# The normalized input of chunks 5 to 7: loaded with columns on partitions and normed on VectorE, in place of transposes on TensorE

## The chip, the cores and the metric

The kernel runs on one core of a Trainium2 chip. The metric is the device time of one execution in microseconds; the time before is the median of three runs. In what follows TensorE is written PE in the profile's rows, VectorE DVE, ScalarE ACT, GpSimd POOL, and SyncE (which here only issues DMAs) SP.

## The reference

A layer norm of the input goes into two branches, and their sum and the input are the result. One branch is a long causal convolution with a gate, the other a dense layer with Mish between two matrix products.

```python
x = A_q                                   # 1 x 2048 x 448
xn = _layernorm(x, axis=-1)               # (x - mean) / sqrt(var + 1e-5)
return x + _A_ref(xn, A_k, A_v, A_shift_k, A_ssm_k, A_ssm_D) + _B_ref(xn, B_w1, B_b1, B_w2)

# A: k_shift = 4-tap causal convolution of k;  kv = k_shift * v
#    y = causal convolution of kv with ssm_k over 2048 steps + kv * ssm_D;  return xn * y
# B: h = xn @ w1 + b1                       # 448 -> 1792
#    return (h * tanh(softplus(h))) @ w2    # 1792 -> 448
```

## The kernel before

**The dense branch** is cut into 8 chunks of 256 tokens, and each chunk into 7 pairs of 128 hidden units. A pair is two slots. In the even slot `g1_mm` multiplies the first layer (L466), in the odd slot `mish` (L469) applies Mish on ScalarE, rounds the result to `ach` and has VectorE subtract the rest, `acl` (L74), and `g2_mm` (L493 to L495) adds the second layer of the pair two earlier to PSUM. Every product is made of rounded high and low parts, 22 matmuls in a first layer and 12 in a second. Chunk c is normalized while chunk c-1 runs, and `g2_evac` (L500) adds the second layer's PSUM to the chunk's own input and SP stores it (L505).

**The norm of a chunk** starts from tokens on partitions: `ln_load` fetches the chunk into `qt`, `ln_stats` queues two `bn_stats`, two `bn_aggr` and the addition of eps for VectorE, and POOL makes 1/sqrt (L395) and the shift. These five small steps are not put in at once: each `dv()` in the program takes one from the list `drip`, so they come between VectorE's other instructions, and what is left is flushed two pairs before the chunk ends. `ln_norm` norms on ScalarE into `xn` (L402), and `ln_T` has TensorE transpose a half of the chunk into PSUM (four matmuls with an identity, L427), ScalarE round it to `XH` (L439) and VectorE subtract the rest, `XL` (L437). The first half is done in the odd slot of pair 5 ahead of that pair's Mish, the second in the even slot of pair 6.

**The convolution branch** is a Fourier transform in two steps of 64 and 32 points, a product and the way back, and its pieces are put into the slots by a table. `f1_mm` (L127) is the 64-point step, `f1_fold` its VectorE part (`st`, L134 and L136), and ScalarE stores the result to `Dkv`. From slot 63 on eight octets follow: SP loads `ah` and `av` back, `h2_mm` and `v2_mm` (L201) are the 32-point step, ScalarE copies their PSUM to `hs` and `vs`, VectorE multiplies (`prod`: `ya`, `yb`, `yc`, `yd`, L234), `i1_mm` (L244) goes back, and `qe` is stored to `E`. From slot 98 on `E` is loaded again (`e`), VectorE folds it (L287, L289), `i2_mm` (L305) makes the result and `gate` multiplies it with the normalized input. `h2_mm`, `v2_mm` and `i1_mm` share two PSUM tiles `pc`, so each waits for ScalarE's copies of the one before.

**The order** on each engine is that of the program; nothing is reordered. Pieces named with `at` come ahead of the dense branch's part of a slot, those with `after` behind it, and `inside` puts some between Mish and `ach` where a transpose shares the slot. A DMA that reads what an earlier DMA wrote waits for its landing on the queue of the engine that issues it, and what stands behind it on this engine waits too.

Of the kernel before, what the change touches and what calls it, by code (L numbers as in the profile page):

```python
# [7 lines left out]
F32 = mybir.dt.float32  # L8
# [6 lines left out]
S, D, F = 2048, 448, 1792  # L15
NJ = 16
NF = F // 128
NP = NF // 2
CH = 256
NCHUNK = S // CH  # L20
# [7 lines left out]
OCT_AT = (65, 3)  # L28
I2_AT = {98: (6, 7), 102: (0, 1), 106: (2, 3), 109: (4, 5)}
LATE = 2  # L30
WARM = (448,) * 4 + (128,)
FILL = ((64,), (128, 128))


@with_exitstack
def tile_kernel(ctx: ExitStack, tc, q, k, v, sk, hT, sD, w1, b1, w2, c_f1, c_g, c_gi, c_i2, out):
    nc = tc.nc
    V = nc.vector

    def pool(name, bufs=1, stack=ctx, **kw):  # L40
        return stack.enter_context(tc.tile_pool(name=name, bufs=bufs, **kw))

    cp = pool("consts")
    wp = pool("weights")
    mp = pool("mlp")
# [3 lines left out]
    dp = pool("scratch", space=DRAM)  # L49
# [4 lines left out]
    Dkv = dp.tile([NO * 16, 32, D], F32, name="Dkv")  # L54
    E = dp.tile([2, 2, 32, 2, NCHUNK, 2, D], F32, name="E")

    f1id = cp.tile([128, 2, 128], F32, name="f1id")
    f1, ident = f1id[:, 0], f1id[:, 1]
    mhalf = cp.tile([128, 2], F32, name="mhalf")
    b1t = cp.tile([128, NF], F32, name="b1t")  # L60
    mv = cp.tile([128, NJ, 2], F32, name="mv")
    rstd = cp.tile([128, NJ], F32, name="rstd")
# [9 lines left out]
    def split(h, l, raw):  # L72
        nc.scalar.copy(h, raw)  # L73
        V.tensor_sub(l, raw, h)  # L74
# [2 lines left out]
        return pcp.tile([128, 2, 512], F32, name="pc")  # L77


    drip = []  # L80

    def dv(n=1):
        for _ in range(n):
            if drip:
                drip.pop(0)()


    plan, plan2, plan3 = {}, {}, {}
# [5 lines left out]
        plan2.setdefault(int(slot), []).append((fn, args))  # L94

    def inside(slot, fn, *args):
        (plan3 if slot % 2 and slot // 2 % NP == NP - 2 else plan2).setdefault(int(slot), []).append((fn, args))


    ph1 = ExitStack()  # L100
    sp1 = pool("ph1", stack=ph1)
    skb = sp1.tile([128, 4, D], F32, name="skb")
    HT, KR, VT, KV, PS, ST, SD = {}, {}, {}, {}, {}, {}, []

    def xt():
# [70 lines left out]
    def t2(shape, name, bufs=1):  # L176
        if not sp2:
            ph1.close()
            sp2.append(ph2.enter_context(tc.tile_pool(name="ph2", bufs=1, reuse_waits="tile")))
        return sp2[0].tile(shape, F32, name=name, bufs=bufs)  # L180
# [85 lines left out]
    def t3(shape, name, bufs=2):  # L266
        if not sp3:
            ph2.close()
            sp3.append(ph3.enter_context(tc.tile_pool(name="ph3", bufs=2, reuse_waits="tile")))
            i2 = sp3[0].tile([128, 2, 32], F32, name="i2", bufs=1)  # L270
            nc.sync.dma_start(i2, c_i2)
            sp3.append(i2)
        return sp3[0].tile(shape, F32, name=name, bufs=bufs)

    def late(c):
        return c >= NCHUNK - LATE

# [88 lines left out]
    XS, XN, NORM = {}, {}, {}  # L366

    def ln_load(c, eng=None):
        Q[c] = mp.tile([128, 2, D], F32, name="qt", tag="qt", bufs=3)
        if c:  # L370
            nc.sync.dma_start(Q[c], q[:, 2 * c:2 * c + 2])
        else:
            for jj in range(2):
                nc.sync.dma_start(Q[c][:, jj], q[:, jj])

    def ln_parts(c):
        st = mp.tile([128, 2, 6], F32, name="bst", bufs=2)
        ve = mp.tile([128, 2], F32, name="ve", bufs=2)
        xn = mp.tile([128, 2, D + 64], F32, name="xn", tag="xn", bufs=1)
        XN[c] = xn  # L380

        def stats(jj):
            V.bn_stats(st[:, jj], Q[c][:, jj])  # L383

        def aggr(jj):
            V.bn_aggr(mv[:, 2 * c + jj], st[:, jj])  # L386

        def eps(a, b):
            V.tensor_scalar(ve[:, a:b], mv[:, 2 * c + a:2 * c + b, 1], EPS, None, op0=ALU.add)

        def power(a, b):
            r, m = (t[:, 2 * c + a:2 * c + b] for t in (rstd, shift))
            if c:
                nc.gpsimd.tensor_tensor(m, mv[:, 2 * c + a:2 * c + b, 0], mone[:, a:b], op=ALU.mult)  # L394
            nc.gpsimd.tensor_tensor(r, ve[:, a:b], mhalf[:, a:b], op=ALU.pow)  # L395
            if c:
                nc.gpsimd.tensor_tensor(m, m, r, op=ALU.mult)

        def norm(jj):
            j = 2 * c + jj  # L400
            if c:
                nc.scalar.activation(xn[:, jj, :D], Q[c][:, jj], AF.Identity, bias=shift[:, j:j + 1],  # L402
                                     scale=rstd[:, j:j + 1])
            else:
                V.tensor_scalar(xn[:, jj, :D], Q[c][:, jj], mv[:, j, 0:1], rstd[:, j:j + 1],
                                op0=ALU.subtract, op1=ALU.mult)

        def tail(a, b):
            (nc.scalar.copy if c else V.tensor_copy)(xn[:, a:b, D:], xn[:, a:b, D - 64:D])

        return stats, aggr, eps, power, norm, tail

    def ln_stats(c):
        stats, aggr, eps, power, norm, tail = ln_parts(c)
        drip.extend([lambda: stats(0), lambda: stats(1), lambda: aggr(0), lambda: aggr(1),
                     lambda: [eps(0, 2), power(0, 2)]])
        NORM[c] = norm, tail

    def ln_norm(c):
        norm, tail = NORM.pop(c)  # L420
        norm(0)
        norm(1)
        tail(0, 2)

    def transposes(c, jj, p):
        for kt in range(4):
            nc.tensor.transpose(p[:, 128 * kt:128 * kt + 128], XN[c][:, jj, 128 * kt:128 * kt + 128], ident)  # L427

    def x_tiles(c):
        XS[c] = (mp.tile([128, 4, CH], F32R, name="XH", tag="XH", bufs=2),  # L430
                 mp.tile([128, 4, CH], F32R, name="XL", tag="XL", bufs=2))
# [9 lines left out]
    def ln_T(c, jj):  # L441
        if jj == 0:
            x_tiles(c)
        p = g1p.tile([128, 2, CH], F32, name="pg1").rearrange("p a b -> p (a b)")
        transposes(c, jj, p)
        for lo in range(2):
            x_split(c, jj, p, lo)
# [5 lines left out]
    def g1_mm(i):  # L453
        c, p = pairs[i]
        XH, XL = XS[c]
        ps = g1p.tile([128, 2, CH], F32, name="pg1")
        for n in range(2):
            f = 2 * p + n
            fs = slice(128 * f, 128 * f + 128)
            mm = []  # L460
            hh, hl, lh = ([(w[:, kt, fs], x[:, kt]) for kt in range(3)] for w, x in ((w1h, XH), (w1h, XL), (w1l, XH)))
            th, tl = ((w1h[:, 3, fs], x[:, 3]) for x in (XH, XL))

            mm = hh + hl + lh + [th, tl] if i == 0 and n else hh + lh + [th] + hl + [tl]
            for n_, (l, r) in enumerate(mm):
                nc.tensor.matmul(ps[:, n], l, r, start=n_ == 0, stop=n_ == len(mm) - 1)  # L466
        P1[i] = ps

    def mish(i, s):  # L469
        p = pairs[i][1]  # L470
        ps = P1.pop(i)
        a = mp.tile([128, 2, CH], F32, name="a", bufs=2)
        for n in range(2):
            nc.scalar.activation(a[:, n], ps[:, n], AF.Mish, bias=b1t[:, 2 * p + n:2 * p + n + 1])  # L474
        for fn, args in plan3.pop(s, ()):
            fn(*args)
        ah = mp.tile([128, 2, CH], F32R, name="ach", bufs=3)
        al = mp.tile([128, 2, CH], F32R, name="acl", bufs=3)
        split(ah, al, a)
        dv()  # L480
        AHL[i] = ah, al
# [25 lines left out]
    def mlp_slot(s):  # L507
        i, half = divmod(s, 2)
        n = len(pairs)
        j = i - G2_LAG  # L510
        if half == 0:
            if i < n:
                c, p = pairs[i]
                if c + 1 < NCHUNK:
                    if p == (0 if c else 1):
                        ln_load(c + 1)
                    if p == (2 if c else 3):
                        ln_stats(c + 1)
                    if c == 0 or p == NP - 3:
                        dv(len(drip))  # L520
                    if p == NP - 2:
                        ln_norm(c + 1)
                    if p == NP - 1:
                        ln_T(c + 1, 1)
                g1_mm(i)
        else:
            if i < n:
                c, p = pairs[i]
                if p == NP - 2 and c + 1 < NCHUNK:
                    ln_T(c + 1, 0)  # L530
                mish(i, s)
            if 0 <= j < n - 1:
                g2_mm(j)
            elif j == n - 1:
                for jj in range(2):
                    g2_mm(j, (jj,))
                    g2_evac(pairs[j][0], (jj,))
# [71 lines left out]

    heat(WARM)  # L610
    ln_load(0)
    nc.scalar.dma_start(f1id, c_f1)
    w1_load(0, ((0, 1, nc.scalar), (1, 2, nc.sync)))
# [26 lines left out]
    for s in range(nslots):  # L640
        j = s // 2 - G2_LAG - 1
# [70 lines left out]
```

## Time and profile before

| | |
|---|---|
| median of 3 runs | 372.51 us (372.32 to 373.36) |
| the profiled execution | 372.71 us, its span 370.3 us |
| instructions | 7465 |
| granted clock of TensorE | 1.000 |

The span runs from the first to the last instruction, and the 2.4 us between it and the execution's own time lie around it. The page cuts the span into 40 slices of 9.26 us; a digit is the busy share in tenths.

```profile
DVE  5798758999999998997432848555384822897741
ACT  4777553543426323533454556557555435235450
DMA  8899989747587427614876497877493329649963
```

VectorE is full up to about 175 us (the taps and the 64-point steps), less so where the octets run, and busy again from 312 us on. In a timeline a row gives the start in us, the length, the engine (PEq, ACTq, SPq for what only issues), the line, what is written and read, and in brackets how long the engine stood idle before it and for whom. Lengths of matmuls overlap: the distance between two starts is what a matmul takes of TensorE. In the list of DMA issues the last number is the time from issue to landing.

### The profile page before, as it was taken

Reading aid. Unit: us, or ns where it says so; the run is one execution under the profiler, and the core shown is the slowest. Engines: PE = TensorE matmul, PEld = TensorE weight load, DVE = VectorE, ACT = ScalarE, POOL = GpSimd, SP = SyncE. Lnnn points to the kernel's source line nnn. Section 1 sums busy time; section 2 is a strip of 40 time slices with the busy share of each in tenths; the row PEclk is TensorE's granted clock in tenths of the full one; section 3 lists DMA queues with packets and bytes.
Section 4 is the critical chain, followed back from the end, with each engine's and each line's share of the span. In section 5 each row is a group of like instructions: output and inputs, shape, how many; then the busy total and the mean of one; then the engine's idle time right before and its main releaser. Section 6 shows DMA issues by size and latency. Waiting matters only on the chain.

```text
span 370.3 us, 7465 instructions
## 1 busy us (share of the span) xinstructions
PE 363.7 (98%) x3136; PEld 294.4 (80%) x3136; DVE 265.8 (72%) x356; ACT 177.0 (48%) x298; POOL 21.9 (6%) x38
## 2 busy tenths in 40 slices
PE   8999999999999999999999999999999999999995
PEld 3888888888888988988886666666666879889884
DVE  5798758999999998997432848555384822897741
ACT  4777553543426323533454556557555435235450
POOL 2010001000020001000010000020000010112110
PEclk9999999999999999999999999999999999999999
DMA  8899989747587427614876497877493329649963
GB/s 285 285 321 337 396 288 270 181 152 238 148 273 228 100 54 247 169 32 99 264 237 218 139 301 239 264 240 242 167 298 116 149 104 364 226 180 298 226 106 94
DMA packets 32354, 79.35 MB, mean 214 GB/s; under 512 B 2881, under 2 KB 18114, under 8 KB 32322
## 3 DMA queue, kind: packets, MB, share of 16 engines
q1 hardware_dynamic: 25986, 57.39, 45.4%
q10 hardware_dynamic: 4896, 15.08, 15.0%
q0 software_dynamic: 1440, 6.42, 7.0%
q8 instruction: 24, 0.39, 0.5%
q14 instruction: 8, 0.07, 0.0%
HBM read 50.44 MB, written 28.44 MB: 213 GB/s over the span
## 4 chain that ended last, share of the span: by engine, by line
PE 83%; DVE 8%; DMA 5%; ACT 1%; issue 1%; POOL 0%; SPq 0%; ACTq 0%
PE pg L466 34%; PE pg L493 11%; PE pg L495 10%; PE pg L494 10%; PE pc L201 7%; PE pc L127 4%; PE pc L244 3%; PE pg L427 2%; PE pc L305 2%; DMA kr<-in_k_dram 2%; DMA Dkv<-st 1%; DMA av<-Dkv 1%; DMA qt<-in_q_dram 1%; DVE x L165 1%; DVE bst L383 1%
## 5 line engine op out<-in xcount | busy, mean ns | idle before, releaser
L474 ACT ACTIVATE a<-pg,b1t 128x256 f32<-128x256 f32 x112 | 47.1, 473 | 108.4 <-PE pg L466 85.0
L466 PE MATMUL pg<-XH,w1h 128*128 128x256 f32 x448 | 91.3, 285 | 0.2
L493 PE MATMUL pg<-w2h,ach 128*128 128x448 f32 x224 | 83.6, 373 | 0.2 <-DVE qt L500 0.2
L466 PEld LDWEIGHTS pg<-XH,w1h 128*128 128x128 f32 x448 | 69.7, 188 | 17.3 <-issue 14.3
L495 PE MATMUL pg<-w2h,acl 128*128 128x448 f32 x224 | 81.3, 363 | 0.0
L494 PE MATMUL pg<-w2l,ach 128*128 128x448 f32 x224 | 81.2, 362 | 0.0
L74 DVE TENSOR_TENSOR acl<-a,ach 128x512 fp32r<-128x512 f32 x56 | 38.5, 687 | 58.7 <-ACT ach L73 58.5
L466 PE MATMUL pg<-XL,w1h 128*128 128x256 f32 x448 | 69.8, 278 | 0.0
L466 PEld LDWEIGHTS pg<-XL,w1h 128*128 128x128 f32 x448 | 59.6, 188 | 0.1
L466 PE MATMUL pg<-XH,w1l 128*128 128x256 f32 x336 | 57.0, 278 | 0.0
L493 PEld LDWEIGHTS pg<-w2h,ach 128*128 128x128 f32 x224 | 42.0, 187 | 14.0 <-issue 9.7
L466 PEld LDWEIGHTS pg<-XH,w1l 128*128 128x128 f32 x336 | 47.0, 188 | 0.0
L495 PEld LDWEIGHTS pg<-w2h,acl 128*128 128x128 f32 x224 | 42.1, 188 | 2.8
L494 PEld LDWEIGHTS pg<-w2l,ach 128*128 128x128 f32 x224 | 42.1, 188 | 2.2
L73 ACT CAST ach<-a 128x512 fp32r<-128x512 f32 x56 | 34.8, 622 | 1.7
L165 DVE TENSOR_TENSOR x<-x 128x896 f32<-128x896 f32 x24 | 26.2, 1090 | 0.8
L439 ACT CAST XH<-pg 128x512 fp32r<-128x512 f32 x16 | 9.4, 588 | 26.5 <-PE pg L427 24.2
L437 DVE TENSOR_TENSOR XL<-pg,XH 128x512 fp32r<-128x512 f32 x16 | 10.9, 684 | 14.4 <-ACT XH L439 14.3
L133 ACT COPY st<-pc 128x896 f32<-128x896 f32 x16 | 14.5, 906 | 13.3 <-PE pc L127 13.3
L134 DVE TENSOR_TENSOR st<-pc,st 128x896 f32<-128x896 f32 x16 | 17.4, 1086 | 4.2 <-ACT st L133 4.0
L394 POOL TENSOR_TENSOR shift<-mv,mone 128x2 f32<-128x2 f32 x7 | 2.8, 397 | 277.9 <-DVE mv L386 277.9
L252 ACT COPY qe<-pc 128x896 f32<-128x896 f32 x16 | 13.8, 913 | 10.8 <-PE pc L244 10.8
(65 smaller groups left out, 392.1 us busy)
## 6 DMA issues: line engine op xcount, KB each, us to landing
Dh<-st ACTq DMA_DIRECT2D x16, 448.0 KB, 5.5
Dkv<-st ACTq DMA_DIRECT2D x16, 448.0 KB, 4.9
ah<-Dh SPq DMA_DIRECT2D x8, 896.0 KB, 6.4
av<-Dkv SPq DMA_DIRECT2D x8, 896.0 KB, 5.4
E<-qe SPq DMA_DIRECT2D x16, 448.0 KB, 3.7
kr<-in_k_dram SPq DMA_DIRECT2D x10, 448.0 KB, 6.1
x<-in_hT_dram SPq DMA_DIRECT2D x8, 448.0 KB, 6.7
x<-in_v_dram SPq DMA_DIRECT2D x8, 448.0 KB, 4.1
```

The source lines that it names most:

```text
L73: nc.scalar.copy(h, raw)
L74: V.tensor_sub(l, raw, h)
L127: nc.tensor.matmul(ps[h][64 * jj:64 * jj + 64, b, :D], f1[rg:rg + 32, 0:64], x[rg:rg + 32, jj], start=True, stop=True, tile_position=(rg, ...
L133: nc.scalar.copy(st[:, 1], o)
L134: V.tensor_add(st[:, 0], e, st[:, 1])
L165: V.tensor_add(KV[g], KV[g], o)
L201: nc.tensor.matmul(p[32 * t:32 * t + 32, r, :D], g[rs, t, c], a[rs, t], start=True, stop=True, tile_position=(64 * r, 32 * t))
L466: nc.tensor.matmul(ps[:, n], l, r, start=n_ == 0, stop=n_ == len(mm) - 1)
L474: nc.scalar.activation(a[:, n], ps[:, n], AF.Mish, bias=b1t[:, 2 * p + n:2 * p + n + 1])
L493: nc.tensor.matmul(ps, ah[:, n, cs], w2h[:, f], start=f == 0, stop=False)
L494: nc.tensor.matmul(ps, ah[:, n, cs], w2l[:, f], start=False, stop=False)
L495: nc.tensor.matmul(ps, al[:, n, cs], w2h[:, f], start=False, stop=f == NF - 1)
```

## The change

Chunks 5, 6 and 7 (`TURN = 5`, `turned(c)`) get their normalized input on another way.

- The input `qx`, made ahead of the launch as a copy of the three chunks with columns on partitions (128 partitions x 4 groups x 256 tokens, 512 KB for a chunk), is loaded by SP into the buffer of `xn`, ahead of `qt`. The chunk is still loaded as `qt` too, for the statistics and for `g2_evac`.
- The statistics are queued one pair earlier (pair 1 in place of 2) and flushed one pair earlier (pair 3 in place of 4). POOL's two shift instructions are left out.
- In the odd slot of pair 3, `ms_store` has ScalarE's queue store mean and 1/sqrt of the 256 tokens to `MS` in memory, two DMAs of 128 x 2 single values. In the odd slot of pair 4, `ms_load` loads them back to all 128 partitions as `bc` (128 x 512, 256 KB). Both stand ahead of the slot's Mish.
- In the odd slot of pair 5, behind Mish and `acl`, `x_norm` subtracts the mean and multiplies by 1/sqrt on VectorE, two instructions of 128 x 1024. In the even slot of pair 6, `x_cast` rounds to `XH` on ScalarE (one instruction of 128 x 1024) and subtracts to `XL` on VectorE (one of 128 x 1024).
- The 24 transposes, the three times three instructions of `ln_norm` and the twelve half-size `XH` and `XL` are gone. The `hs` or `qe` copies that stood between Mish and `ach` in pair 5 now stand behind the slot.
- The transform's matrix and the identity move to a memory pool that is closed before the octets start.

```diff
+TURN = 5
...
+    MS = dp.tile([NCHUNK, 2, CH], F32, name="MS")
...
     def inside(slot, fn, *args):
-        (plan3 if slot % 2 and slot // 2 % NP == NP - 2 else plan2).setdefault(int(slot), []).append((fn, args))
+        c, p = divmod(slot // 2, NP)
+        (plan3 if slot % 2 and p == NP - 2 and not turned(c + 1) else plan2).setdefault(int(slot), []).append((fn, args))
...
     def ln_load(c, eng=None):
+        if turned(c):
+            XN[c] = mp.tile([128, 4, CH], F32, name="xt", tag="xn", bufs=1)
+            nc.sync.dma_start(XN[c], qx[:, c - TURN])
...
+    def ms_store(c):
+        for i, t in enumerate((mv[:, 2 * c:2 * c + 2, 0], rstd[:, 2 * c:2 * c + 2])):
+            nc.scalar.dma_start(MS[c, i].rearrange("(j p) -> p j", p=128), t)
+
+    def ms_load(c):
+        BC[c] = t3([128, 2, CH], "bc", 1) if c == NCHUNK - 1 else t2([128, 2, CH], "bc")
+        nc.scalar.dma_start(BC[c], MS[c].partition_broadcast(128))
+
+    def x_norm(c):
+        for i, op in enumerate((V.tensor_sub, V.tensor_mul)):
+            op(XN[c], XN[c], BC[c][:, i:i + 1].to_broadcast([128, 4, CH]))
+
+    def x_cast(c):
+        x_tiles(c)
+        split(*XS[c], XN[c])
...
-                    if p == (2 if c else 3):
+                    if p == ((1 if turned(c + 1) else 2) if c else 3):
                         ln_stats(c + 1)
-                    if c == 0 or p == NP - 3:
+                    if c == 0 or p == (NP - 4 if turned(c + 1) else NP - 3):
                         dv(len(drip))
-                    if p == NP - 2:
+                    if turned(c + 1):
+                        if p == NP - 1:
+                            x_cast(c + 1)
+                    elif p == NP - 2:
                         ln_norm(c + 1)
-                    if p == NP - 1:
+                    elif p == NP - 1:
                         ln_T(c + 1, 1)
...
-                if p == NP - 2 and c + 1 < NCHUNK:
+                t = turned(c + 1) and c + 1 < NCHUNK
+                if t and p == NP - 4:
+                    ms_store(c + 1)
+                if t and p == NP - 3:
+                    ms_load(c + 1)
+                if p == NP - 2 and c + 1 < TURN:
                     ln_T(c + 1, 0)
                 mish(i, s)
+                if t and p == NP - 2:
+                    x_norm(c + 1)
```

The order moves at three places that the prediction speaks of. In these rows a line number of the changed program is 7 to 28 higher than before for the same statement.

The first is VectorE in slots 59 to 62, where chunk 5 is being prepared: `acl` is the dense branch's subtraction, `qt` the emptying of chunk 3's second layer, `st` the last 64-point step, `bst`, `mv` and `ve` the statistics of chunk 5. Before:

```order
L74 TENSOR_TENSOR acl<-a,ach 128x512 x2
L500 TENSOR_TENSOR qt<-pg_1653,qt 128x448
L500 TENSOR_TENSOR qt<-pg_1657,qt 128x448
L134 TENSOR_TENSOR st<-pc,st 128x896
L383 BN_STATS bst<-qt 128x6
L136 TENSOR_TENSOR st<-pc,st 128x896
L383 BN_STATS bst<-qt 128x6
L74 TENSOR_TENSOR acl<-a,ach 128x512
```

Now:

```order
L75 TENSOR_TENSOR acl<-a,ach 128x512 x2
L393 BN_STATS bst<-qt 128x6
L528 TENSOR_TENSOR qt<-pg_1654,qt 128x448
L393 BN_STATS bst<-qt 128x6
L528 TENSOR_TENSOR qt<-pg_1658,qt 128x448
L396 BN_AGGR mv<-bst 128x2
L141 TENSOR_TENSOR st<-pc,st 128x896
L396 BN_AGGR mv<-bst 128x2
L143 TENSOR_TENSOR st<-pc,st 128x896
L399 TENSOR_SCALAR ve<-mv 128x2
```

Both statistics have moved from between the folds to ahead of the second add.

The second is VectorE in slots 87 to 90, with octet 7's product (`ya` to `yc`), the emptying of chunk 5 and the statistics of chunk 7. Before:

```order
L74 TENSOR_TENSOR acl<-a,ach 128x512
L234 TENSOR_TENSOR ya<-vs,hs 128x896
L234 TENSOR_TENSOR yb<-vs,hs 128x896
L234 TENSOR_TENSOR ya<-ya,yb 128x896
L500 TENSOR_TENSOR qt<-pg_2694,qt 128x448
L500 TENSOR_TENSOR qt<-pg_2698,qt 128x448
L234 TENSOR_TENSOR yc<-vs,hs 128x896
L383 BN_STATS bst<-qt 128x6
L234 TENSOR_TENSOR yd<-vs,hs 128x896
L383 BN_STATS bst<-qt 128x6
L234 TENSOR_TENSOR yc<-yc,yd 128x896
L386 BN_AGGR mv<-bst 128x2
```

Now:

```order
L393 BN_STATS bst<-qt 128x6
L241 TENSOR_TENSOR ya<-vs,hs 128x896
L393 BN_STATS bst<-qt 128x6
L241 TENSOR_TENSOR yb<-vs,hs 128x896
L396 BN_AGGR mv<-bst 128x2
L241 TENSOR_TENSOR ya<-ya,yb 128x896
L396 BN_AGGR mv<-bst 128x2
L528 TENSOR_TENSOR qt<-pg_2691,qt 128x448
L399 TENSOR_SCALAR ve<-mv 128x2
L528 TENSOR_TENSOR qt<-pg_2695,qt 128x448
L241 TENSOR_TENSOR yc<-vs,hs 128x896
L241 TENSOR_TENSOR yd<-vs,hs 128x896
```

All of the statistics, the aggregations and eps too, have come ahead of the last `yc`.

The third is VectorE in slots 93 to 97, where chunk 7 is made ready and chunks 6 and 7 of the convolution are folded (`ex`, `e`). Before:

```order
L437 TENSOR_TENSOR XL<-pg_3536,XH 128x4x128
L74 TENSOR_TENSOR acl<-a,ach 128x512
L287 TENSOR_TENSOR ex<-e_3500 128x896
L289 TENSOR_TENSOR e_3500<-e_3500 128x896
L287 TENSOR_TENSOR ex<-e_3502 128x896
L289 TENSOR_TENSOR e_3502<-e_3502 128x896
L437 TENSOR_TENSOR XL<-pg_3570,XH 128x4x128
L74 TENSOR_TENSOR acl<-a,ach 128x512
```

Now:

```order
L75 TENSOR_TENSOR acl<-a,ach 128x512 x4
L447 TENSOR_TENSOR xt<-xt,bc 128x1024 x2
L294 TENSOR_TENSOR ex<-e_3484 128x896
L296 TENSOR_TENSOR e_3484<-e_3484 128x896
L294 TENSOR_TENSOR ex<-e_3486 128x896
L296 TENSOR_TENSOR e_3486<-e_3486 128x896
L75 TENSOR_TENSOR XL<-xt,XH 128x1024
L75 TENSOR_TENSOR acl<-a,ach 128x512
```

Two instructions of 1024 columns that wait for `bc` stand ahead of the four folds, and one `XL` of 1024 columns behind them, in place of a half one on either side.

More of the change, by code (lines that the diff above doesn't have):

```diff
@@ L35, in tile_kernel @@
 @with_exitstack
-def tile_kernel(ctx: ExitStack, tc, q, k, v, sk, hT, sD, w1, b1, w2, c_f1, c_g, c_gi, c_i2, out):
+def tile_kernel(ctx: ExitStack, tc, q, qx, k, v, sk, hT, sD, w1, b1, w2, c_f1, c_g, c_gi, c_i2, out):
     nc = tc.nc
@@ L55, in tile_kernel @@
     E = dp.tile([2, 2, 32, 2, NCHUNK, 2, D], F32, name="E")
-    f1id = cp.tile([128, 2, 128], F32, name="f1id")
-    f1, ident = f1id[:, 0], f1id[:, 1]
+    MS = dp.tile([NCHUNK, 2, CH], F32, name="MS")
     mhalf = cp.tile([128, 2], F32, name="mhalf")
@@ L77, in pc, with turned @@
         return pcp.tile([128, 2, 512], F32, name="pc")
+    def turned(c):
+        return c >= TURN
     drip = []
@@ L102, in tile_kernel @@
     skb = sp1.tile([128, 4, D], F32, name="skb")
+    f1id = sp1.tile([128, 2, 128], F32, name="f1id")
+    f1, ident = f1id[:, 0], f1id[:, 1]
     HT, KR, VT, KV, PS, ST, SD = {}, {}, {}, {}, {}, {}, []
@@ L378, in ln_parts @@
         ve = mp.tile([128, 2], F32, name="ve", bufs=2)
-        xn = mp.tile([128, 2, D + 64], F32, name="xn", tag="xn", bufs=1)
-        XN[c] = xn
+        if not turned(c):
+            XN[c] = xn = mp.tile([128, 2, D + 64], F32, name="xn", tag="xn", bufs=1)
         def stats(jj):
@@ L392, in power @@
             r, m = (t[:, 2 * c + a:2 * c + b] for t in (rstd, shift))
-            if c:
+            if c and not turned(c):
                 nc.gpsimd.tensor_tensor(m, mv[:, 2 * c + a:2 * c + b, 0], mone[:, a:b], op=ALU.mult)
             nc.gpsimd.tensor_tensor(r, ve[:, a:b], mhalf[:, a:b], op=ALU.pow)
-            if c:
+            if c and not turned(c):
                 nc.gpsimd.tensor_tensor(m, m, r, op=ALU.mult)
@@ L423, in ln_norm @@
         tail(0, 2)
+    BC = {}
+    def ms_store(c):
[10 more added lines that the diff above has]
+        split(*XS[c], XN[c])
     def transposes(c, jj, p):
@@ L693 @@
     lay = lambda x: x.reshape(32, 2, 2, 16, D).transpose(2, 1, 0, 3, 4).reshape(128, NJ, D)
+    qx = lay(a["A_q"][0])[:, :, np.r_[0:D, D - 64:D]].reshape(128, NCHUNK, 2, 4, 128)[:, TURN:]
     kpad = np.pad(a["A_k"][0], ((4, 0), (0, 0)))
     arrs = dict(
-        q=lay(a["A_q"][0]), k=np.concatenate([lay(kpad[:S])[:, :, :][:, :4], lay(a["A_k"][0])], axis=1),
+        q=lay(a["A_q"][0]), qx=qx.transpose(4, 1, 3, 2, 0).reshape(128, NCHUNK - TURN, 4, CH), k=np.concatenate([lay(kpad[:S])[:, :, :][:, :4], lay(a["A_k"][0])], axis=1),
         v=lay(a["A_v"][0]), sk=a["A_shift_k"].T, hT=lay(a["A_ssm_k"].T), sD=a["A_ssm_D"][None],
```

## The prediction

> **What bounds the kernel now.** I read the page's busy times and its chain of waits first, then the timelines of each engine around the three places where chunks 5, 6 and 7 are prepared, then the DMA landings.
>
> ```profile
> PE 363.7 (98%) x3136; PEld 294.4 (80%) x3136; DVE 265.8 (72%) x356; ACT 177.0 (48%) x298; POOL 21.9 (6%) x38
> PE 83%; DVE 8%; DMA 5%; ACT 1%; issue 1%; POOL 0%; SPq 0%; ACTq 0%
> ```
>
> TensorE sets the time: it is nearly never idle and holds 83% of the chain that ended last. So whatever leaves TensorE's own order is gained, and a longer VectorE or a DMA costs only where TensorE then waits. VectorE's 8% and DMA's 5% of the chain say that there are such places; they lie just where this change moves work.
>
> **What is removed: 24 transposes.** Each chunk from 5 on loses two groups of four. The timeline of TensorE shows a group at chunk 5 and one at chunk 7, each with the row after it.
>
> ```profile
> 198.96 0.65 PE L427 MATMUL pg<-f1id,xn 128*128 128x128 f32 x4
> 199.37 0.45 PE L493 MATMUL pg<-w2h,ach 128*128 128x448 f32 x1
> ...
> 310.77 0.60 PE L427 MATMUL pg<-f1id,xn 128*128 128x128 f32 x4
> 311.13 0.45 PE L493 MATMUL pg<-w2h,ach 128*128 128x448 f32 x1
> ```
>
> Matmuls overlap, so what counts is from start to start: 0.41 us, and 0.36 us in chunk 7. Four times 0.41 and twice 0.36 are **2.36 us off** TensorE.
>
> **Two waits in chunks 5 and 6 that should go.** ScalarE now casts XH only after the transposes, and the Mish of that pair stands behind the cast. In the new order Mish runs as soon as its matmuls end, so the whole VectorE queue behind it starts earlier. The chain of waits shows what that is worth: the inverse step i1_mm (32 matmuls at L244), late at octet 0, normal at octet 1, late at octet 5. The two ScalarE rows show why.
>
> ```profile
> 206.88 2.49 PE pc L244 x32
> 220.63 1.69 PE pc L244 x32
> 273.39 2.08 PE pc L244 x28
> ...
> 205.87 1.71 ACT L221 COPY vs<-pc 128x896 f32<-128x896 f32 x2 [0.96 <-DVE yd L234]
> 271.97 1.72 ACT L221 COPY vs<-pc 128x896 f32<-128x896 f32 x2 [1.33 <-DVE yd L234]
> ```
>
> i1_mm needs the two PSUM tiles that those vs copies free, and the copies wait for VectorE's yd. The excess over 1.69 is 0.80 and 0.39 us. Is yd earlier now, though x_norm stands ahead of it?
>
> ```profile
> L74 DVE TENSOR_TENSOR acl<-a,ach 128x512 fp32r<-128x512 f32 x56 | 38.5, 687 | 58.7 <-ACT ach L73 58.5
> L165 DVE TENSOR_TENSOR x<-x 128x896 f32<-128x896 f32 x24 | 26.2, 1090 | 0.8
> ...
> 197.30 1.73 PE L201 MATMUL pc<-ah,g 64*32 64x448 f32 x32
> 306.06 0.84 ACT L474 ACTIVATE a<-pg,b1t 128x256 f32<-128x256 f32 x2 [3.42 <-PE pg L466]
> 307.58 0.69 DVE L74 TENSOR_TENSOR acl<-a,ach 128x512 fp32r<-128x512 f32 x1 [4.13 <-ACT ach L73]
> ```
>
> No row has 128x1024; from 687 ns for 512 and 1090 for 896 the slope is 1.05 ns a column, so about 1.22 us, and 1.15 in a row of others. The first part of x_norm to XL is 2.4 us for the two, XL another 1.15. The first layer of that pair ends at 197.30 (the next matmul starts); Mish to acl takes 1.52 (306.06 to 307.58), so acl stands at 198.9, x_norm at 199.5 to 201.9, and yd ends near 204.0 instead of 205.84. The vs copies end near 205.7, and TensorE, 0.82 earlier, comes at 206.0: the wait is gone with 0.3 to spare. In chunk 6 the same sum frees the tiles at 272.4 against an arrival at 272.5: gone, barely. I take **1.19 off**; the ends are 0 and 1.19. XL is ready at 206.4 and 268.7, some 6 us ahead of its first use, so x_norm, cast and XL are hidden there.
>
> **What is moved: the statistics, one pair earlier.** At chunk 5 they now stand ahead of and between the two adds that empty the second layer's PSUM (the first piece of order above). Behind those adds SP's queue waits.
>
> ```profile
> 174.63 1.15 DVE L500 TENSOR_TENSOR qt<-pg,qt 128x448 f32<-128x448 f32 x2
> ...
> 177.86 0.62 DVE L383 BATCH_NORM_STATS2 bst<-qt 128x6 f32<-128x448 f32 x1
> 178.39 1.07 DVE L136 TENSOR_TENSOR st<-pc,st 128x896 f32<-128x896 f32 x1
> ```
>
> ```profile
> 175.81 0.34 SPq L505 DMA_DIRECT2D out_dram<-qt  x1
> ...
> 176.72 0.59 SPq L188 DMA_DIRECT2D ah<-Dh  x1
> ...
> ah<-Dh SPq DMA_DIRECT2D x1, 896.0 KB, 6.4
> ...
> DMA to landing us min/median/max: 4.7/6.4/7.7
> ...
> 183.36 1.73 PE L201 MATMUL pc<-ah,g 64*32 64x448 f32 x32
> 190.50 1.74 PE L201 MATMUL pc<-av,g 64*32 64x448 f32 x32 [0.21 <-DMA av<-Dkv]
> ```
>
> The store of chunk 3 is issued as the second add ends, and the load ah of octet 0 stands behind it. It lands at 183.12 (176.72 + 6.4) for matmuls at 183.36: 0.24 us of slack. Two statistics of 0.53 (177.86 to 178.39) put all three issues 1.06 later; ah then lands at 184.18 and TensorE waits 0.82. By the extremes of ah's row the wait is 0 (4.7) to 2.1 (7.7). The Dkv stores now overlap ah more, since their last fold has lost the statistics that stood between, so I take **1.2 on**. The 0.21 wait for av goes, being covered: **0.21 off**. In chunk 6 the moved statistics cost nothing: there the chain of waits runs over TensorE alone, and VectorE has idle time ahead of each acl; without that cover they would be another 1.06.
>
> At octet 7 VectorE is the chain itself.
>
> ```profile
> 297.25 0.17 DVE L386 BATCH_NORM_AGGREGATE mv<-bst 128x2 f32<-128x6 f32 x1
> 297.34 0.66 DVE L74 TENSOR_TENSOR acl<-a,ach 128x512 fp32r<-128x512 f32 x1
> ...
> 297.39 1.01 PE L244 MATMUL pc<-yc,gi 32*64 32x448 f32 x16 [0.41 <-DVE yc L234]
> ```
>
> Two aggregations and the eps addition, about 0.09 each (297.25 to 297.34), now come ahead of the yc for which TensorE waits: **0.27 on**.
>
> **What is added: the trip through memory, and chunk 7.** ms_load waits on ScalarE's queue for both stores, with a Mish behind it. In chunks 5 and 6 two long pairs lie between the stores and x_norm, and nothing is late. In chunk 7 the pairs are short. The stores go out behind the copies of octet 7 (298.44 + 1.72), by 301.3 with two issues of 0.59 each as in ah's row, and x_norm could start at 313.0: 11.7 us for two landings and an issue. The rows nearest to them, behind that of the copies:
>
> ```profile
> 298.44 1.72 ACT L252 COPY qe<-pc 128x896 f32<-128x896 f32 x2 [3.27 <-PE pc L244]
> ...
> i<-in_c_i_dram SPq DMA_DIRECT2D x1, 32.0 KB, 2.6
> Dkv<-st ACTq DMA_DIRECT2D x16, 448.0 KB, 4.9
> q<-in_q_dram SPq DMA_DIRECT2D x3, 448.0 KB, 10.9
> ```
>
> Two of 4.9 and the issue land at 311.7, with 1.3 to spare; the bounds are 2.6 twice and 4.9 with 10.9 (a load issued behind four of 896 KB, as bc is). I take 4.9, the row of ScalarE's own queue: no cost. The Mish held behind ms_load is needed two pairs later.
>
> But VectorE has no slack from there on.
>
> ```profile
> 313.42 0.69 DVE L74 TENSOR_TENSOR acl<-a,ach 128x512 fp32r<-128x512 f32 x1 [0.70 <-ACT ach L73]
> 314.03 1.08 DVE L287 TENSOR_TENSOR ex<-e 128x896 f32<-128x896 f32 x1
> 318.28 0.68 DVE L437 TENSOR_TENSOR XL<-pg,XH 128x512 fp32r<-128x512 f32 x1
> 330.50 0.68 DVE L74 TENSOR_TENSOR acl<-a,ach 128x512 fp32r<-128x512 f32 x1
> ...
> 319.15 0.57 PE L305 MATMUL pc<-ex,i 64*32 64x448 f32 x2
> 330.84 0.57 PE L305 MATMUL pc<-ex,i 64*32 64x448 f32 x2
> ```
>
> acl comes at 312.4 (310.77 + 0.1 + 1.52), x_norm ends at 315.4, the folds (4.25) at 319.65 where they ended at 318.28, XL at 320.8. TensorE, 0.72 earlier, wants the second of two fold results at 319.26 and waits 0.45. The queue stays full to the next folds, which end at 331.7 instead of 330.5: another 0.4. So the 0.72 of chunk 7 is handed back: **0.8 on**; between 0 and 1.5.
>
> **Sum:** -2.36 - 1.19 + 1.2 - 0.21 + 0.27 + 0.8 = -1.5 us. The profiled execution took 372.71 (span 370.3 and 2.4 around it), 0.2 above the median of 372.51; against its own time that gives **371.2**.
>
> **Rivals.** First, slower: bc of chunk 7 comes late and takes the place of the transposes' wait. Every microsecond past 313.0 stops VectorE's full queue and so TensorE. At 10.9 after an issue at 306.2 it lands at 317.1: +4.1, that is 375.3. It turns into a loss from 314.5, 8.3 us after the issue. For it: the loads e and q fill the DMA engines then; against it: bc is on ScalarE's queue, and the Dkv stores on it moved data while ah on SP's was still moving.
>
> ```profile
> q1 hardware_dynamic: 182, 0.30, 78.9%
> q10 hardware_dynamic: 34, 0.12, 29.8%
> ```
>
> That is 181 to 182 us: the queue of ScalarE (q10) got a share beside SP's (q1). [...]
>
> Second, no change: ah lands at 185.5 (7.7 after 177.78), +0.9, and the wait of octet 0 stays, because the copies of vs end too late, +0.8: 372.9.
>
> Third, more gain: ah comes in time after all and VectorE's backlog in chunk 7 doesn't reach TensorE: -1.2 - 0.8 more, 369.2.
>
> That the transposes are not saved is excluded by the order: TensorE loses just these 24 rows.
>
> **How the numbers follow.** The forecast 0.58 (370.2 to 372.3), the late bc 0.14, the eaten gain 0.18, the full gain 0.10. 0.3% of 372.51, about what a measurement of this kernel can tell from no change, is 1.1 us: faster is below 371.4. Of the forecast 0.35 lies there: faster 0.45, same 0.23 + 0.18 = 0.41, slower 0.14. Range 369.8 to 373.4: it leaves out the late bc and a part of the full gain.
>
> **What would show it.** Right: TensorE waits about 1 us ahead of the first L201 matmuls, i1_mm of octets 0 and 5 takes 1.7, i1_mm of octet 7 still waits for yc, and the two first pairs of i2_mm wait for the folds. Wrong: x_norm of chunk 7 waits for bc, ScalarE stands at ms_load so long that TensorE waits for a Mish, or the first L201 doesn't wait.

## The result and the profile after

The changed kernel takes **384.5 us** (median of 4 runs, 383.54 to 386.33) against 372.64 us for the kernel before: 1.033 times the time, with a 95% interval from 1.030 to 1.035. The forecast of 371.2 was wrong, and the time lies far outside its range. The profiled execution took 383.83 us, its span is 381.7.

The page of the changed kernel: busy times by engine, the granted clock in 40 slices, and the chain that ended last by engine.

```profile
PE 364.7 (96%) x3112; PEld 292.7 (77%) x3112; DVE 272.5 (71%) x359; ACT 172.9 (45%) x286; POOL 19.6 (5%) x32
PEclk9999999999999999999978999999999999999999
PE 75%; DMA 17%; DVE 5%; ACT 2%; issue 1%; SPq 0%; ACTq 0%; POOL 0%
```

TensorE lost its 24 transposes (3136 to 3112 instructions). Its busy time is nevertheless 1 us longer than before, because some matmuls ran at a lowered clock (the 7 and 8 in the slices; 0.989 in the mean). The DMA's part of the chain went from 5% to 17%: 18.5 us before (0.05 x 370.3), 64.9 after. VectorE, which got the new work, went from 8% to 5%. So the time was lost in waits for transfers. Which ones, the pieces of the chain of waits show (start, length, what):

```profile
179.65 12.34 DMA Dkv<-st
192.01 5.37 DMA av<-Dkv
...
247.55 11.91 DMA ah<-Dh
261.42 12.26 DMA ah<-Dh
...
309.82 11.83 DMA E<-qe
321.73 5.56 DMA e<-E
```

In the place of the first two, the kernel before has these; for E its list of issues gives the median to landing (ah took 4.7 to 7.7 there):

```profile
180.11 5.24 DMA Dkv<-st
185.44 4.93 DMA av<-Dkv
```

```profile
E<-qe SPq DMA_DIRECT2D x16, 448.0 KB, 3.7
```

None of the late transfers, Dkv, ah and E at near 12 us, belongs to the change. They are the convolution's own stores and loads. What they have in common is the time: Dkv, the first ah and E are in flight beside the stores of mean and scale, which stand on ScalarE's queue (start, duration of the issue):

```profile
180.32 2.32 ACTq L439 DMA_DIRECT2D MS<-mv  x1
182.73 1.59 ACTq L439 DMA_DIRECT2D MS<-rstd  x1
...
192.43 0.35 ACTq L443 DMA_DIRECT2D bc<-MS  x1
...
247.56 0.44 ACTq L439 DMA_DIRECT2D MS<-mv  x1
248.10 0.47 ACTq L439 DMA_DIRECT2D MS<-rstd  x1
...
261.94 0.34 ACTq L443 DMA_DIRECT2D bc<-MS  x1
```

bc is issued when its stores have landed: 12.1 us after the first of them in chunk 5 (180.32 to 192.43) and in chunk 7 (307.59 to 319.69), 14.4 in chunk 6 (247.56 to 261.94). The second ah is another case. It is issued at 261.42, half a microsecond before the stores of chunk 6 have landed, and is in flight beside bc. With the stores alone (e2 below) the ah in its place took 7.4 us in place of 12.26.

TensorE's timeline shows what the late transfers cost at octet 0 (the row's last part is the idle time before it and what ended it):

```profile
183.89 1.74 PE L208 MATMUL pc<-ah,g 64*32 64x448 f32 x32 [0.86 <-DMA ah<-Dh]
197.51 3.24 PE L208 MATMUL pc<-av,g 64*32 64x448 f32 x32 [6.76 <-DMA av<-Dkv]
```

The same 32 matmuls of av took 1.74 before; 3.24 is the lowered clock behind the wait (0.50 from 196 to 202 us). Read as starts of the same matmuls, after minus before, the time went as follows:

| matmuls | before | after | difference |
|---|---|---|---|
| ah of octet 0 | 183.36 | 183.89 | +0.53 |
| av of octet 0 | 190.50 | 197.51 | +7.01 |
| ah of octet 1 | 197.30 | 206.78 | +9.48 |
| av of octet 4 | 242.28 | 250.10 | +7.82 |
| ah of octet 6 | 264.27 | 273.81 | +9.54 |
| i1_mm of octet 7, second half | 297.39 | 306.39 | +9.00 |
| second pair of i2_mm | 330.84 | 342.85 | +12.01 |
| span | 370.3 | 381.7 | +11.4 |

Four fifths of the loss (9.48 of 12.01) arise at octet 0, within 23 us. The gains that were forecast are there (9.48 to 7.82 behind it), but small beside it.

A small part comes from a wait for the stores themselves. In chunk 6 ScalarE stands at ms_load until they land; Mish and the hs copies stand behind it, and TensorE waits for these:

```profile
262.32 0.84 ACT L502 ACTIVATE a<-pg,b1t 128x256 f32<-128x256 f32 x2 [3.44 <-DMA MS<-rstd]
...
264.67 1.79 PE L208 MATMUL pc<-av,g 64*32 64x448 f32 x32 [0.73 <-ACT hs L219]
```

### The profile page after: what moved, and what is told of

The parts are those of the page before. It is cut to its first block, busy times and chain, and to the rows that moved or that the text cites. A ratio compares the mean times of both kernels' runs of the same rounds, so it can differ in the third digit from the quotient of the medians.

```text
span 381.7 us, 7421 instructions
## 1 busy us (share of the span) xinstructions
PE 364.7 (96%) x3112; PEld 292.7 (77%) x3112; DVE 272.5 (71%) x359; ACT 172.9 (45%) x286; POOL 19.6 (5%) x32
## 2 busy tenths in 40 slices
DMA packets 34851, 81.73 MB, mean 214 GB/s; under 512 B 4609, under 2 KB 19842, under 8 KB 34818
## 4 chain that ended last, share of the span: by engine, by line
PE 75%; DMA 17%; DVE 5%; ACT 2%; issue 1%; SPq 0%; ACTq 0%; POOL 0%
PE pg L494 31%; PE pg L521 10%; PE pg L523 9%; PE pg L522 9%; DMA ah<-Dh 6%; PE pc L208 6%; PE pc L134 4%; DMA Dkv<-st 3%; DMA E<-qe 3%; PE pc L251 2%; PE pc L312 2%; DMA e<-E 1%; DMA av<-Dkv 1%; PE pg L455 1%; DMA qt<-in_q_dram 1%; ACT a L502 1%
## 5 line engine op out<-in xcount | busy, mean ns | idle before, releaser
L494 PEld LDWEIGHTS pg<-XH,w1h 128*128 128x128 f32 x448 | 69.7, 188 | 18.5 <-issue 15.8
L521 PEld LDWEIGHTS pg<-w2h,ach 128*128 128x128 f32 x224 | 42.2, 188 | 16.9 <-issue 11.9
L208 PE MATMUL pc<-av,g 64*32 64x448 f32 x256 | 15.4, 594 | 7.5 <-DMA av<-Dkv 6.8
L228 ACT COPY vs<-pc 128x896 f32<-128x896 f32 x16 | 13.8, 910 | 12.5 <-PE pc L208 9.9
L241 DVE TENSOR_TENSOR ya<-vs,hs 128x896 f32<-128x896 f32 x8 | 8.7, 1087 | 13.3 <-PE pc L251 8.1
```

Of the source, the lines that this page charges most:

```text
L208: nc.tensor.matmul(p[32 * t:32 * t + 32, r, :D], g[rs, t, c], a[rs, t], start=True, stop=True, tile_position=(64 * r, 32 * t))
L521: nc.tensor.matmul(ps, ah[:, n, cs], w2h[:, f], start=f == 0, stop=False)
```

## The experiments

Theory A: the stores, 2 x 256 packets of 4 bytes a chunk, make everything that is in flight beside them late. (The pages count 2881 packets under 512 bytes before and 4609 after, 1728 more; by their shapes the six stores are 1536 of these.) Its rivals, B and C in the first expectations, hold that those stores disturb nobody else: TensorE is held by what waits for the trip's data (bc and x_norm), or by the rest of the change. "Before" below means runs of the kernel before on the same chip in the same sitting: 372.4 to 372.6 us.

**e1, no stores.** The broadcast load stays and reads rows of an input; mean and scale are thus not the right ones.

```diff
-                if t and p == NP - 4:
-                    ms_store(c + 1)
...
-        nc.scalar.dma_start(BC[c], MS[c].partition_broadcast(128))
+        nc.scalar.dma_start(BC[c], qx[0, c - TURN, 0:2].partition_broadcast(128))
```

> Leaves out the two stores of mean and scale; bc is loaded at the same place and size from an input, so the values normed with are not the reference's. Theory A (the 256 four-byte packets of each store hold the DMA engines, and other transfers with them): the 12 us landings of Dkv, ah and E vanish, 370.5 to 372.5. Theory B (ScalarE's queue standing at ms_load is the cost): the same, since nothing is waited for. Theory C (the added loads of qx and bc crowd the engines): stays above 380.

Measured: 375.37 us (374.64 to 375.74), ratio 1.0069 [1.0042, 1.0097]. Nine of the twelve microseconds are gone with the stores, as theory A wants, but 3 us more are left than it expected. e6 says why.

**e2, the stores alone,** in the kernel before; nobody reads what they write.

```diff
+                if p == NP - 4 and 5 <= c + 1 < NCHUNK:
+                    for k in range(2):
+                        nc.scalar.dma_start(MS[c + 1, k].rearrange("(j p) -> p j", p=128), b1t[:, 2 * k:2 * k + 2])
```

> The kernel before, with the changed kernel's two stores at the same places for chunks 5 to 7 (of two columns of b1t, into memory that nothing reads). Nobody waits for them. Theory A: Dkv ahead of octet 0 lands some 7 us late, ah of octet 5 or 6 about 1 us, E of octet 7 some 8 us: 379 to 384. Theory B and theory C: 372.6.

Measured: 385.57 us (385.03 to 386.88), ratio 1.035 [1.032, 1.038]. Six stores of 1 KB, read by no one, cost 13.2 us (385.57 less 372.41), more than the whole loss of 11.9, and more than the 379 to 384 that theory A expected. Nobody waits for them here, so a wait for their data is not needed for such a loss; the 0.73 us above are a small part of the changed kernel's. TensorE's timeline shows the wait of octet 0 again:

```profile
197.62 3.24 PE L202 MATMUL pc<-av,g 64*32 64x448 f32 x32 [7.59 <-DMA av<-Dkv]
```

**e3, rows instead of columns:** the changed kernel with the same number of stores and bytes, but each store is two rows of 512 bytes, taken from the input tile (so mean and scale are not the right ones).

```diff
-        for i, t in enumerate((mv[:, 2 * c:2 * c + 2, 0], rstd[:, 2 * c:2 * c + 2])):
-            nc.scalar.dma_start(MS[c, i].rearrange("(j p) -> p j", p=128), t)
+        for i in range(2):
+            nc.scalar.dma_start(MS[c, i].rearrange("(j p) -> j p", p=128), Q[c][0:2, i, 0:128])
```

> The changed kernel with the same two stores of 1 KB at the same places, but each of two rows of 512 bytes (of the chunk's input, so not the reference's values) in place of 256 single values; ms_load waits for them as before. Theory A: landings of 2 to 5 us, 370.5 to 372.5. Theory B, if any trip through memory is too long for the wait on ScalarE: 375 to 384.

Measured: 373.91 us (371.99 to 374.93, 10 runs), ratio 1.0021 [0.9997, 1.0044]. The trip through memory, the waits for it and the queue are all there. What differs is the stores' packets, 4 of 512 bytes from two partitions in place of 512 of 4 bytes from 128, and 10.6 us are gone (384.5 less 373.91). Theory A's range is still missed by 1.4. e3 loads bc beside av as e1 does, and TensorE waits for av:

```profile
193.55 3.24 PE L208 MATMUL pc<-av,g 64*32 64x448 f32 x32 [2.49 <-DMA av<-Dkv]
```

The ten runs go with TensorE's clock: the four with a mean granted clock of 0.998 to 1.000 took 372.0 to 373.1 us, the six with 0.994 or 0.995 took 373.9 to 374.9.

**e4, half the packets:** mean and scale side by side, one store of 256 packets of 8 bytes a chunk, the same bytes. POOL puts the scale beside the mean, and bc is loaded and read in this order.

```diff
-        for i, t in enumerate((mv[:, 2 * c:2 * c + 2, 0], rstd[:, 2 * c:2 * c + 2])):
-            nc.scalar.dma_start(MS[c, i].rearrange("(j p) -> p j", p=128), t)
+        nc.scalar.dma_start(MS[c].rearrange("(j p) i -> p j i", p=128), mv[:, 2 * c:2 * c + 2])
```

> The changed kernel with mean and scale of a token side by side: one store of 256 packets of 8 bytes for a chunk in place of two of 256 packets of 4, the same bytes. Theory A, if packets count: the landing falls from 12 to about 6 us, and the time to 375 to 378. If bytes count: 384. Theory B: between 374 and 378, by the shorter wait.

Measured: 377.55 us (375.19 to 378.26), ratio 1.012 [1.008, 1.016]. That lies in theory A's range and in theory B's, so the time alone does not choose between them. The landing of the store fell from 12.1 to 7.7 us in chunk 5, less than theory A had (about 6). The store of Dkv at octet 0 decides; it stands here in the chains of e3 and e4:

```profile
179.96 6.34 DMA Dkv<-st
```

```profile
181.07 8.24 DMA Dkv<-st
```

It took 6.1 us without such stores (e1), 6.3 beside 4 packets (e3), 8.2 beside 256 (e4) and 12.3 beside 512. The bytes of the stores are the same in the last three, so it is the packets and not the bytes: above e3, 3.6 us are left of 10.6 with half of them. Whether their number or their small size counts these runs don't separate, since at the same bytes one goes with the other. e3's rows of 512 bytes cost nothing against e1 (373.91 us against 375.37), packets of 8 and of 4 bytes do (377.55 and 384.5); by what mechanism no run here shows.

**e5, one pair of the same stores at a quiet place** of the kernel before: at 281 us, after which no other transfer is issued until 291.5.

```diff
+                if (c, p) == (6, 1):
+                    for k in range(2):
+                        nc.scalar.dma_start(MS[k].rearrange("(j p) -> p j", p=128), b1t[:, 2 * k:2 * k + 2])
```

> The kernel before with ONE pair of the 4-byte stores (2 x 256 packets, of b1 columns, read by nobody) issued on ScalarE's queue at about 281.4 us, behind octet 4's hs copies. In the trace of before nothing is in flight there until E<-qe at 290.3. Theory A (the tiny writes hold the DMA engines, and cost only what other transfers in flight lose): nobody to hold up, 372.3 to 373.0. Rival D (such stores cost TensorE time wherever they stand, a third of the 13 us that six of them cost): 376 to 377.5.

Measured: 372.2 us (371.9 to 374.89, 12 runs), ratio 0.9991 [0.9973, 1.0008]. One such pair made TensorE wait 7.59 us at octet 0 in e2, and costs nothing that can be measured here: the price is what others in flight lose. How long a pair takes by itself, and what the DMA engines do meanwhile, show the issues (KB each, median us to landing) and the windows (last three columns: granted clock, busy share of the DMA engines, GB/s):

```profile
MS<-b1t ACTq DMA_DIRECT2D x2, 1.0 KB, 8.1
```

```profile
281.00:283.00 2.00, 2.00 (x18) 1.88 (x11) 2.00 (x3) 1.54 (x2) 0.00 (x0) 1.00 0.83 217
283.00:287.00 4.00, 4.00 (x51) 2.51 (x50) 1.74 (x2) 1.72 (x2) 0.00 (x0) 1.00 0.01 0
```

In the first window the engines still move a store of E and a load of gi that were issued before the pair; both land in normal time (3.9 and 3.7 us). The pair lands after 8.1 us, and for most of that time the engines are idle by the profile: 0.01 busy. This mends theory A's wording. Here the packets don't occupy the engines; what takes long is the time until they count as landed. In the changed kernel it looks the same at octet 0, where TensorE comes to wait for av and av for Dkv<-st (first row). In its chunk 6 it does not (the other two, ahead of the stall and in it): the engines are 0.70 busy there, but move only 116 GB/s, where 0.85 busy moved 322 just before.

```profile
186.00:192.00 6.00, 4.75 (x34) 4.42 (x32) 0.59 (x1) 1.48 (x2) 0.00 (x0) 1.00 0.00 0
```

```profile
244.00:248.00 4.00, 4.00 (x46) 2.43 (x46) 3.96 (x5) 2.13 (x4) 0.00 (x0) 1.00 0.85 322
252.00:260.00 8.00, 7.23 (x75) 5.34 (x82) 3.60 (x4) 3.13 (x4) 0.00 (x0) 1.00 0.70 116
```

So beside such stores other transfers either stand or go slowly. What holds them up no row shows. It is not one queue alone that is late: in the changed kernel Dkv<-st on ScalarE's own queue took 12.34 us, the first ah and E<-qe on SP's 11.91 and 11.83.

**e6, no trip at all:** the changed kernel without stores and load. x_norm reads a resident tile, so mean and scale are not the right ones.

```diff
-                if t and p == NP - 4:
-                    ms_store(c + 1)
-                if t and p == NP - 3:
-                    ms_load(c + 1)
...
-            op(XN[c], XN[c], BC[c][:, i:i + 1].to_broadcast([128, 4, CH]))
+            op(XN[c], XN[c], Q[c][:, i:i + 1, :CH].to_broadcast([128, 4, CH]))
```

> The changed kernel without stores and without the broadcast load: x_norm's second operand is the resident qt, so the whole trip through memory is left out and everything else of the change stays. Theory R1 (what is left over in e1 is the 256 KB broadcast load that shares the engines with av of octet 0: av 7.5 us instead of 4.9): the wait for av falls from 2.9 to under 1 us, the granted clock stays at 1, and the time is 371.3 to 372.4. Rival R2 (the left-over comes from the statistics' new place, that is from ah's later issue, which lands beside Dkv<-st): the wait stays at 2 to 3 us and the time at 374 to 375.4.

Measured: 370.09 us (369.63 to 370.59), ratio 0.9928 [0.9911, 0.9946]. It is still less than the 371.3 that theory R1 gave as the lower end. So the left-over of e1 is the broadcast load: with it 375.37, without it 370.09. The chain of e1 shows the load av, beside which bc is issued, and the chain of e6 the same load without bc:

```profile
179.72 6.11 DMA Dkv<-st
185.85 7.52 DMA av<-Dkv
```

```profile
179.91 6.14 DMA Dkv<-st
186.07 4.76 DMA av<-Dkv
```

256 KB of bc make the 896 KB of av 2.8 us longer. TensorE's timeline in e1 and in e6:

```profile
193.50 2.36 PE L208 MATMUL pc<-av,g 64*32 64x448 f32 x32 [2.88 <-DMA av<-Dkv]
```

```profile
190.97 1.74 PE L208 MATMUL pc<-av,g 64*32 64x448 f32 x32 [0.21 <-DMA av<-Dkv]
```

2.7 us more of waiting, 0.6 on these matmuls and more on the next, since the clock is still down (0.57 in the mean from 194 to 198 us): in e1 the av matmuls of octet 0 start 3.00 us later than before and the ah matmuls of octet 1 4.59 later; in e6 the two are 0.47 and 0.53 later. In the changed kernel bc costs less at this place: there it goes out behind av (192.43 after 192.01), and av took 5.37.

**e7, the order alone:** the kernel before, with Mish ahead of the first half's evictions for chunks 5 and 6. It tests the forecast's 1.19 by itself.

```diff
+                t = p == NP - 2 and c + 1 in (5, 6)
-                if p == NP - 2 and c + 1 < NCHUNK:
+                if p == NP - 2 and c + 1 < NCHUNK and not t:
                     ln_T(c + 1, 0)
                 mish(i, s)
+                if t:
+                    ln_T(c + 1, 0)
```

> The kernel before with one edit: for chunks 5 and 6 Mish and its split stand ahead of the first half's transposes' evictions (XH, XL) instead of behind them. This is the 1.19 us of the prediction by itself (i1_mm waits 0.80 at octet 0 and 0.39 at octet 5 because ScalarE's cast stands ahead of Mish). If ScalarE's order is what makes yd late: 371.3 to 371.9. Rival: XL, now behind acl but still ahead of yc and yd on VectorE (0.69 us), takes the gain back: 372.3 to 372.7.

Measured: 371.51 us (370.91 to 373.23, 12 runs), ratio 0.9973 [0.9960, 0.9985]: 0.98 us of the 1.19 by the medians (372.49 less 371.51). Its chain has i1_mm of octets 0 and 5 at the normal length:

```profile
208.09 1.69 PE pc L244 x32
...
273.80 1.69 PE pc L244 x32
```

**e8, a version with rows that computes the reference:** only chunks 6 and 7 turned; TensorE transposes the 128 x 4 statistics, ScalarE copies them, and the store is four packets of 512 bytes. x_norm becomes four instructions of half the size.

```diff
-TURN = 5
+TURN = 6
...
     def ms_store(c):
+        p = g1p.tile([128, 2, CH], F32, name="pg1")
+        nc.tensor.transpose(p[:4, 0, :128], mv[:, 2 * c:2 * c + 2].rearrange("p j i -> p (j i)"), ident)
+        r = mp.tile([128, 2, CH], F32, name="a", bufs=2)[:4, 0, :128]
+        nc.scalar.copy(r, p[:4, 0, :128])
+        nc.scalar.dma_start(MS[c].rearrange("j i r -> (j i) r"), r)
```

> A version that computes the reference: only chunks 6 and 7 are turned, and mean and scale are first transposed by TensorE (one 128x4 transpose a chunk), so that the store is 4 packets of 512 bytes. Theory A: no packet cost; gains of four groups of transposes (0.41 + 0.41 + 0.36 + 0.36) and 0.39 at octet 5, less 0.2 for the two small transposes and 0.6 for yc of octet 7: 371.2 to 372.2. Rival: the small transposes take a PSUM buffer of the first layer's rotation and TensorE waits for it or for POOL's scale: 373 to 375.

Measured: 373.64 us (372.55 to 376.88, 12 runs), ratio 1.0034 [1.0011, 1.0057]. The time lies in the rival's range, but neither theory had the reason. The timelines of ScalarE and TensorE show it:

```profile
244.80 0.26 ACT L443 COPY a<-pg 4x128 f32<-4x128 f32 x1 [3.54 <-PE pg L441]
```

```profile
248.00 1.41 PE L251 MATMUL pc<-ya,gi 32*64 32x448 f32 x12 [0.82 <-ACT vs L228]
```

The small copy waits for a transpose that stands behind the av matmuls in TensorE's order. Mish and the vs copies wait behind it in ScalarE's, and TensorE for these.

**e9, the same with the store behind the vs copies,** and Mish first for chunk 5 as in e7.

```diff
-                if t and p == NP - 4:
-                    ms_store(c + 1)
...
+    for c in range(TURN, NCHUNK):
+        after(2 * ((c - 1) * NP + NP - 4) + 1, ms_store, c)
```

> e8 with two places moved: the small transpose, its copy and the row store stand behind Mish, its split and the vs copies of that slot (in e8 ScalarE's copy waited 3.54 us for the transpose, Mish and vs behind it, and i1_mm waited 0.82 us and came 1.69 later), and for chunk 5, which keeps its transposes, Mish stands first as in e7. Theory: e8's 373.6 less 1.7 and less 0.8: 371.0 to 372.0, so a little better than before and about level with e7. Rival: the store, now later, makes the broadcast load or x_norm late and ScalarE's queue waits behind the load: 372.5 to 374.

Measured: 371.25 us (370.23 to 374.24, 12 runs), ratio 0.9977 [0.9955, 1.0000]: as expected, and level with e7, which is the smaller edit and surer. Both are faster than the changed kernel. Of the two only e7 is clearly faster than the kernel before: its interval lies below 1, that of e9 ends at 1.0000. And since e9 contains e7's edit for chunk 5, what the turned chunks gain by themselves in a kernel that computes the reference is not shown.

## Why the prediction was wrong

**The step that failed** is the one on the trip through memory: "In chunks 5 and 6 two long pairs lie between the stores and x_norm, and nothing is late." The first half is true. But it asks only who waits for the stores, and not who travels beside them. The stores cost most in chunk 5, where they have the most time, since Dkv<-st, av and ah of the first octet are in flight there. e2 shows that they do so when nobody waits for them (13.2 us), e5 that they cost nothing where nobody is in flight. The second half is not even true of the waits: in chunk 6 the stores took so long (14.4 us to bc) that TensorE waited 0.73 us for ScalarE behind ms_load.

**What the text had in hand.** It had a rival in which the trip takes longer and the time goes to 375.3, but it put that cost on bc in chunk 7 alone. Landings from rows of 32 and 448 KB (2.6 to 10.9 us) were taken as bounds for 256 packets of 4 bytes: the nearest by size, but not by packet. For the landing of chunk 7's stores it took 4.9; they took 12.1 us from the first issue to bc.

**The second omission** is bc itself, 256 KB issued beside av. It was costed only as something that lands in time. By e1 and e6 it is worth 5.3 us (375.37 less 370.09), of which the traces show 4.06 at octet 0 (4.59 less 0.53). That is its price where no slow stores hold av up. The prices of stores and bc don't add up to the changed kernel's loss: 13.2 and 5.3, less the 2.4 that e6 gains, are 16.1, and it lost 11.9.

**The rest of the sum** can be read from e6, in which the trip is missing and all else is there. Its differences between starts of the same matmuls, beside the forecast's terms:

| step | forecast | e6 |
|---|---|---|
| ah of octet 0 late | +1.2 | +0.52 |
| wait for av of octet 0 covered | -0.21 | -0.05 (it stays) |
| chunk 5: transposes and i1_mm (2 x 0.41 and 0.80) | -1.62 | -1.66 |
| chunk 6: transposes and i1_mm (2 x 0.41 and 0.39) | -1.21 | -1.17 |
| yc of octet 7 behind the statistics | +0.27 | +0.26 |
| chunk 7: transposes and VectorE's backlog (-0.72 and +0.8) | +0.08 | -0.03 |

The last two are taken at the second half of i1_mm of octet 7 (2.04 early in e6) and at the second pair of i2_mm (2.07 early); the span ends 2.4 early. So the removed transposes, the two waits and chunk 7 came out as worked out, and the two waits also by themselves in e7. At octet 7 the number came out, but at another place. The statistics now stand ahead of the emptying of the second layer's PSUM (qt) too; TensorE waits for that one, ahead of i1_mm, and the wait for yc, 0.41 before, is no longer in the timeline:

```profile
291.62 0.47 PE L521 MATMUL pg<-w2h,ach 128*128 128x448 f32 x1 [0.29 <-DVE qt L528]
```

Only the delay of ah was half of what was taken: the wait is there (0.60 in e6, 0.86 after), but the forecast had raised its 0.82 to 1.2 for an overlap that the runs don't show (ah landed 6.1 us after its issue in e6, and the forecast had 6.4). Without the trip the sum of -1.5 would have been too cautious by 0.9.

**The rival of the late bc** named chunk 7 and 4.1 us. Chunk 7 did lose: from +9.00 at i1_mm of octet 7 to +12.01 at the second pair of i2_mm, 3.0 net, in spite of the transposes saved there. VectorE's timeline shows x_norm waiting for bc at last:

```profile
324.79 2.49 DVE L447 TENSOR_TENSOR xt<-xt,bc 128x1024 f32<-128x1024 f32 x2 [1.04 <-DMA bc<-MS]
```

But the chain goes over E<-qe (11.83) and e, not over bc: again a transfer of others. And chunk 7 was a quarter of the loss.

## What to carry to other kernels

Cost a DMA by what is in flight beside it, not only by who waits for it, and count its packets, not its bytes: here a column of 256 elements written to memory was 256 packets, and two such columns, 2 KB in all, delayed the transfers issued around them by far more than their size would suggest (Dkv<-st of octet 0 took 12.34 us beside them, 6.1 in e1 without). If statistics must cross partitions, turn them into rows first, or place the store where nothing else is in flight. And look whether part of a change's gain is a matter of order alone: here one moved call gave about 1 us, where the whole change gave 2.4 with its trip through memory left out.

## What the runs showed of the hardware that was not expected

- 512 packets of 4 bytes land 8.1 us after issue with no transfer issued beside them (e5), 10.2 us at the median beside other transfers (e2). Meanwhile the DMA engines' busy share can be near 0 (0.01 in e5, 0.00 at octet 0 of the changed kernel) or high at a low rate (0.70 at 116 GB/s in chunk 6). A low share of the DMA engines was thus no sign that transfers were free to go.
- Behind three waits of TensorE, of 6.76 us in the changed kernel, 2.88 in e1 and 2.49 in e3, its matmuls ran slower for some microseconds, so that these waits cost more than their length. In the changed kernel the clock was 0.50 from 196 to 202 us and 1.00 again from 203 on, in e1 it was 0.57 from 194 to 198; in e3 the 32 matmuls of av took 3.24 us, as in the changed kernel, in place of 1.74. The chain of waits from av of octet 0 to the next octet's matmuls, of the changed kernel and of the kernel before (start, length, what):

```profile
197.51 3.24 PE pc L208 x32
...
206.85 0.49 PE pc L208
```

```profile
190.50 1.74 PE pc L201 x32
...
197.37 0.87 PE pc L201 x9
```

It is the same work with no wait in it: 9.34 us (197.51 to 206.85) where it took 6.87 (190.50 to 197.37), so the wait of 6.76 cost another 2.5. The windows show the granted clock (the third column from the end) behind that wait, and in e1 behind the wait of 2.88:

```profile
196.00:200.00 4.00, 2.49 (x32) 0.76 (x32) 0.00 (x0) 0.65 (x1) 0.00 (x0) 0.50 0.93 252
```

```profile
194.00:198.00 4.00, 4.00 (x38) 2.23 (x22) 2.20 (x3) 1.82 (x2) 0.00 (x0) 0.57 0.44 117
```
